# Moving a split, a tail transpose, thresholds and reciprocals in a fused attention and MLP kernel

## The chip, the cores and the metric

The kernel runs on one core of a Trainium2 chip. A core has five engines with instruction queues of their own: TensorE (PE in the profile; its weight loads are PEld), VectorE (DVE), ScalarE (ACT), GpSimd (POOL) and SyncE (SP, which here only issues transfers). Data lies in SBUF and PSUM, 128 partitions each; transfers to and from HBM and transposing transfers run on 16 DMA engines. The metric is the device time of one execution in microseconds (us).

## The reference

Eight batches of eight heads, 576 positions, head size 64. Scores below the row's maximum less `tau` (0.02) are cut off, the rest goes through a softmax and multiplies `v`; the heads are joined, and a two-layer MLP follows:

```python
scores = scale * np.matmul(q, k.transpose(0, 1, 3, 2))          # 8 x 8 x 576 x 576
thresh = np.max(scores, axis=-1, keepdims=True) - tau
scores = np.where(scores >= thresh, scores, -1e9)
attn = np.exp(scores - np.max(scores, axis=-1, keepdims=True))
attn = attn / (np.sum(attn, axis=-1, keepdims=True) + 1e-09)
out = np.matmul(attn, v)                                        # -> x: 4608 x 512
h = x @ w_in                                                    # 512 x 2048
return np.maximum(0.01 * h, h) @ w_out                          # 2048 x 512
```

## The kernel before

**Data.** `q` and `k` come as fp32 and are split into two fp16 parts, a high one (64 times the value, rounded) and a low one (what is left), so that the scores are the sum of three fp16 products (high by high, low by high, high by low). A unit of this work is one batch, one pair of heads and `q` or `k`: a tile `raw` of 128 x 512 elements. The 512 first positions of a batch are its main part; the 64 last ones of all heads are its *tails*, loaded as the tile `rawt` of 128 x 256.

**Splitting.** There are two ways. `split_pool` (L496) does it on POOL alone: scale (L137), cast to the high part (L143), subtract (L147). `split_now` (L150) does it on ACT (high, L157) and DVE (low, L158), in two instructions each per unit. After the split, `turn` (L161) transposes the 16 (for tails 8) blocks on PE into a PSUM tile `tp` with the tag "h", of which there are two buffers, and copies them by ACT or DVE into `kT` or `qT` (L179, L187). The first 64 columns of `kT` are tails, and a second copy of them goes to columns 576 to 640 (L184 for batch 0). `turn_rows` (L189) is the form for batches 2 to 7.

**Steps.** The attention is cut into 144 steps (18 per batch): 128 query rows of a pair of heads, or the tail rows of two pairs. One turn of the loop (L531) handles the scores of step n, the softmax of step n-1, the turning of the weights of earlier steps, and the MLP work that is queued (`l1q`, `l2q`: at most one `layer1` unit and two `layer2` units in a turn). Each engine executes its instructions in the order in which the program issues them. Within a turn:

- PE: `scores` (L244); `idle` matmuls on the identity in the first eleven turns (L505, they fill time and nothing reads them); the transposes of `turn` listed for that turn in `turns_at`; for the first eight steps the transposes of the weights (L323); `layer1` (L383), `layer2` (L399); the product with `v` of an earlier step, `pv` (L340).
- DVE: `copy_min` (L252, two instructions: scores out of PSUM, negated, with the row minimum as an accumulator), the threshold for n < 28 (L261), `weights` of step n-1 (L296: mask times exponential, with the row sum), the reciprocal of the sums (L302), copies out of PSUM, and x, the product with the reciprocal (L362).
- ACT: for one head the exponential (L287), for the other Prelu with the threshold as bias, then the exponential (L283, L284); L385 after `layer1`, L405 after `layer2`.
- POOL: what `pool_at` lists for the turn (splits, casts of `v`, weight loads `load_w`), the threshold for n >= 28 (L264), and `widen` (L305), which spreads the reciprocal to 64 columns for each head. Before turn 7, `widen` runs on DVE.
- SP: loads, stores, and from the ninth step on the transposing transfer of the weights of a pair of steps (L313), right after `widen`; the product with `v` follows three turns or more after the pair's `widen`.

**Start.** Before the loop, the first unit of `k` is loaded from SP's queue and the first of `q` from ACT's. The k tails follow on SP's queue as two transfers, then the second pair and all others. 34 `idle` matmuls run; `first` is the order of batch 0's units: (pair 0, k), (pair 0, q), (tails, k), (1, k), (1, q), (2, k), (2, q), (3, k), (3, q), (tails, q). The first three are split by `split_now` and turned ahead of the loop, with four `idle` matmuls before the tails. The second pair (1, k) and (1, q) is split by `split_now` in turn 0, between step 0's copies and step 1's. POOL splits (2, k) and (2, q) ahead of the loop, (3, k) and (3, q) in turns 0 and 1, the q tails in turn 6:

```python
for key in first[5:7]:
    split_pool(key)
for n_, key in zip((0, 1, 6), first[7:]):
    at(pool_at, n_, lambda key=key: split_pool(key))
for i in range(8):
    at(pool_at, 2 + i // 2 if i < 4 else i, lambda i=i: load_w(i))
```

**Reciprocals.** For the first eight steps the sums of each step are inverted alone (`n == 1` in `recip`). From then on it is once per pair of steps (`n == 2`, 128 x 4 elements), 68 times in all, on DVE, and POOL widens the result.

Of the kernel before, what the change touches and what calls it, by code (L numbers as in the profile page):

```python
# [37 lines left out]
def kernel(  # L38
# [24 lines left out]
    ident = sb.tile([128, 128], FP16, name="ident")  # L63
    minus_tau = sb.tile([128, 1], FP32, name="minus_tau")


# [15 lines left out]

    def load_tails(b, which, eng=None):
        t = sb.tile([128, 2, 2, 64], FP32, tag="rawt", bufs=2, name="rawt")
        src = SRC[which][b, :, MAIN:S, :].rearrange("(u sh) p d -> u p sh d", u=2)
        for u in range(2):
            (eng or nc.sync).dma_start(out=t[ds(64 * u, 64), :, :, :].rearrange("p s h d -> p (s h) d"), in_=src[u])
        tails[b, which] = t
# [61 lines left out]
    def split_now(key):  # L150
        t = halves[key] = new_half()
        for i in range(2):
            if key[1] == "t":
                src, n = tails[key[0], key[2]][:, :, i, :], 2
            else:
                src, n = pair_of(*key)[:, i, :, :], 4
            nc.scalar.activation(out=t[:, 0, 0:n, i, :], in_=src, func=AF.Copy, bias=0.0, scale=64.0)  # L157
            nc.vector.scalar_tensor_tensor(out=t[:, 1, 0:n, i, :], in0=src, scalar=64.0, in1=t[:, 0, 0:n, i, :],  # L158
                                           op0=AX.mult, op1=AX.subtract)

    def turn(key, copy=None):  # L161
        copy = copy or nc.scalar.copy
        b, p, which = key
        dst, half = turned_of(b, which), halves.pop(key)
        n = 2 if p == "t" else 4
        c0 = 0 if which == "q" else 64
        if p == "t":
            c0 = MAIN if which == "q" else 0
            tp = ps.tile([128, 2, 2, 2, 64], FP16, tag="h", bufs=2, name="tp")
        else:  # L170
            tp = ps.tile([128, 2, 4, 128], FP16, tag="h", bufs=2, name="tp")
        for x in range(2):
            for t in range(n):
                for h in range(2):
                    o = tp[ds(64 * h, 64), x, :, t, :] if p == "t" else tp[ds(64 * h, 64), x, t, :]
                    nc.tensor.transpose(o, half[:, x, t, h, :], ident[:, :])
        if p == "t":
            for x in range(2):
                copy(out=dst[:, x, :, ds(c0, 64)], in_=tp[:, x, :, :, :].rearrange("d u s p -> d (u s) p"))  # L179
            if which == "k" and b:  # L180
                nc.gpsimd.tensor_copy(out=dst[:, :, :, 576:640], in_=dst[:, :, :, 0:64])
            elif which == "k":
                for x in range(2):
                    nc.vector.tensor_copy(out=dst[:, x, :, 576:640],  # L184
                                          in_=tp[:, x, :, :, :].rearrange("d u s p -> d (u s) p"))
        else:
            copy(out=dst[:, :, p, ds(c0, 512)], in_=tp[:, :, :, :].rearrange("d x t p -> d x (t p)"))  # L187
# [68 lines left out]
    def threshold(st):  # L256
        st.th = sb.tile([128, 2, 2], FP32, tag="th", bufs=3, name="th")
        if st.n < 28:

            least = sb.tile([128, 1], FP32, tag="least", bufs=2, name="least")  # L260
            nc.vector.tensor_scalar(out=st.th[:, :, 0], in0=st.mn[:, :, 0], scalar1=tau_f, scalar2=None, op0=AX.add,  # L261
                                    op1=AX.min, accum_out=least[:, :])
        else:
            nc.gpsimd.tensor_scalar(out=st.th[:, :, 0], in0=st.mn[:, :, 0], scalar1=1.0, scalar2=tau_f, op0=AX.mult,  # L264
                                    op1=AX.add)
# [34 lines left out]
    def recip(pr, c, n):  # L300
        pr.rec = sb.tile([128, 2, 2], FP32, tag="rec", bufs=2, name="rec")
        nc.vector.reciprocal(out=pr.rec[:, 0:n, :], in_=pr.sum[:, ds(c, n), :])  # L302

# [157 lines left out]
    masks.make_identity(nc, ident[:, :])  # L461
    nc.gpsimd.memset(minus_tau[:, :], -tau_f)

    def load_pair(p, which, eng):
# [6 lines left out]
    load_pair(0, "q", nc.scalar)  # L471
    load_tails(0, "k", nc.sync)
    load_pair(1, "k", nc.sync)
# [4 lines left out]
    for s in range(2):  # L478
        load_v(0, s)
        if s == 0:  # L480
            load_vtails(0)
    load_tails(0, "q", nc.sync)
    for t in v16:
# [29 lines left out]
    turn(first[1], nc.vector.tensor_copy)  # L513
    idle(4)
    turn(first[2])
    idle(5)
    for key in first[5:7]:
        split_pool(key)
    for n_, key in zip((0, 1, 6), first[7:]):
        at(pool_at, n_, lambda key=key: split_pool(key))  # L520
    for i in range(8):
        at(pool_at, 2 + i // 2 if i < 4 else i, lambda i=i: load_w(i))
    at(turns_at, 0, lambda: turn(first[3]))
    for n_, key in zip((1, 2, 3, 4, 8), first[5:]):
        at(turns_at, n_, lambda key=key: turn(key, nc.vector.tensor_copy if key[2] == "q" else None))
# [5 lines left out]
    while n < N + 7 or l1q or l2q or stores:  # L531
# [8 lines left out]
        if n == 0:  # L540
            split_now(first[3])
            threshold(steps[0])
            split_now(first[4])
        if n == 1:
# [72 lines left out]
```

## Time and profile before

| | before |
|---|---|
| median of 3 runs | 500.94 us (500.85 to 500.95) |
| profiled execution | 500.9 us, span 499.1 us |
| PE busy | 475.7 us, 95% |
| DVE busy | 414.3 us, 83% |
| ACT busy | 433.1 us, 87% |
| POOL busy | 305.5 us, 61% |
| granted TensorE clock, mean | 0.996 |
| time of the DMA packets, queue q1 (loads, stores, transposes) | 80.5% of 16 engines |

The profile is of one execution. A line such as `L252 DVE TENSOR_SCALAR_CACHE_REDUCE s<-sc 128x576` names the program line, the engine, the operation, output and input tiles and shape; then come busy time and the mean duration of one in ns, and the idle time of the engine just before with what ended it. In an answer in order of time the first two numbers are the start and the length in us, and a bracket gives the idle time before with what ended it. `DVE_READ_ACCUMULATOR` and `ACTIVATION_READ_ACCUMULATOR` are the second half of an instruction that also gives a sum or a minimum. In a table of stages the numbers are the engine's busy time in that stage, and PEclk is the granted clock, 1.00 at full speed. The chain of waits is followed back from the last instruction, at each step to what released it.

### The profile page before, as it was taken

What the parts mean: (1) busy time and instruction counts of PE and PEld (TensorE: products, weight loads), DVE (VectorE), ACT (ScalarE), POOL (GpSimd) and SP (SyncE); (2) the same over time, 40 slices, a digit from 0 to 9 for tenths busy, and PEclk for the clock granted to TensorE, in tenths of its full rate; (3) what the DMA queues carried; (4) which work ended last, traced back from release to release, by engine and by line L of the source; (5) the groups of instructions that cost most, each with busy time, mean ns of one, the idle gap of its engine ahead of it and who ended that gap; (6) DMA issues with size and microseconds to landing.
All of it is one profiled execution on the core that took longest, in us unless ns stands there. A gap on an engine that the chain in (4) does not pass through costs nothing.

```text
span 499.1 us, 19695 instructions
## 1 busy us (share of the span) xinstructions
PE 475.7 (95%) x8043; PEld 344.4 (69%) x8043; DVE 414.3 (83%) x1228; ACT 433.1 (87%) x785; POOL 305.5 (61%) x517
## 2 busy tenths in 40 slices
PE   7878789989999999999999999999999999999996
PEld 6556566656677777777777777777777777667884
DVE  4999999998989898998989898998989898878100
ACT  4998987898999999999999999999999999999431
POOL 4973687557867687666867687666867683322000
PEclk9989999999999999999999999999999999999999
DMA  8897898899998999999997999999898969767512
GB/s 246 238 202 121 156 193 175 144 205 189 217 168 182 193 204 211 186 165 220 191 185 172 203 199 199 195 172 210 197 200 153 205 148 158 138 117 144 126 45 65
DMA packets 220443, 87.79 MB, mean 176 GB/s; under 512 B 190656, under 2 KB 217280, under 8 KB 220352
## 3 DMA queue, kind: packets, MB, share of 16 engines
q1 hardware_dynamic: 217392, 82.07, 80.5%
q0 software_dynamic: 2688, 4.19, 4.8%
q8 instruction: 63, 1.03, 0.9%
q10 hardware_dynamic: 272, 0.26, 0.2%
q14 instruction: 28, 0.23, 0.1%
HBM read 36.70 MB, written 9.44 MB: 92 GB/s over the span
## 4 chain that ended last, share of the span: by engine, by line
PE 80%; DVE 11%; ACT 3%; DMA 2%; issue 1%; POOL 1%; SPq 0%; DVEq 0%; POOLq 0%; ACTq 0%
PE hp L383 26%; PE o L399 20%; PE sc L244 20%; PE pv L340 7%; DVE s L252 5%; PE osc L399 3%; DVE w L296 3%; PE tpr L199 3%; DMA wT<-w 2%; DMA rawt<-in_k_dram 1%; DVE x L362 1%; ACT wT L325 1%; ACT s L283 1%; DVE half L158 1%; ACT e L287 1%
## 5 line engine op out<-in xcount | busy, mean ns | idle before, releaser
L252 DVE TENSOR_SCALAR_CACHE_REDUCE s<-sc 128x576 f32<-128x576 f32 x288 | 206.4, 754 | 32.6 <-PE sc L244 31.4
L244 PE MATMUL sc<-kT,qT 64*128 64x288 f16 (+1 forms) x1920 | 135.8, 286 | 4.0 <-DVE s L252 3.2
L383 PE MATMUL hp<-x,win 128*64 128x256 f16 x2048 | 136.5, 275 | 1.1 <-DVE x L362 1.0
L383 PEld LDWEIGHTS <-win 128*64 128x64 f16 x2560 | 118.5, 109 | 24.0 <-issue 18.1
L399 PE MATMUL o<-wout,g 128*64 128x512 f16 x992 | 127.8, 379 | 0.0
L296 DVE SCALAR_TENSOR_TENSOR w<-s,th,e 128x576 f16<-128x576 f32 x144 | 122.2, 849 | 0.5 <-ACT e L287 0.5
L244 PEld LDWEIGHTS <-qT 64*128 64x128 f16 (+1 forms) x1920 | 77.0, 97 | 58.6 <-issue 44.2
L264 POOL TENSOR_SCALAR th<-mn 128x2 f32<-128x2 f32 x116 | 53.5, 461 | 103.3 <-DVE s L252 76.9
L284 ACT ACTIVATE w<-s,minus_tau 128x576 f16<-128x576 f32 x144 | 111.7, 776 | 5.2
L283 ACT ACTIVATE s<-s,th 128x576 f32<-128x576 f32 x144 | 110.4, 766 | 2.0 <-POOL th L264 1.4
L287 ACT ACTIVATE e<-s,mn 128x576 f16<-128x576 f32 x144 | 110.2, 766 | 0.6 <-DVE s L252 0.5
L385 ACT ACTIVATE g<-hp 128x512 f16<-128x512 f32 x144 | 84.2, 585 | 29.3 <-PE hp L383 28.8
L399 PEld LDWEIGHTS <-g 128*64 128x64 f16 x1152 | 65.1, 110 | 30.1 <-issue 0.5
L147 POOL TENSOR_TENSOR half<-scaled,half 128x512 f16<-128x512 f32 (+1 forms) x75 | 82.2, 1096 | 1.1
L340 PE MATMUL pv<-wT,v 128*64 128x256 f16 (+1 forms) x960 | 52.1, 247 | 2.6 <-DMA wT<-w 2.6
L340 PEld LDWEIGHTS <-v 128*64 128x64 f16 x960 | 41.6, 111 | 15.8 <-issue 3.0
L137 POOL TENSOR_SCALAR scaled<-raw 128x512 f32<-128x512 f32 x60 | 43.7, 728 | 7.1 <-DMA raw<-in_k_dram 6.1
L305 POOL CAST w<-rec 128x256 f16<-128x256 f32 (+1 forms) x70 | 27.9, 398 | 31.4 <-DVE rec L302 31.0
L143 POOL CAST half<-scaled 128x512 f16<-128x512 f32 (+1 forms) x75 | 43.2, 576 | 4.6
L106 POOL CAST v<-vraw 128x256 f16<-128x256 f32 x64 | 34.4, 565 | 1.4
L362 DVE TENSOR_TENSOR x<-pv,wT 128x256 f16<-128x256 f32 x64 | 27.1, 423 | 3.5 <-PE pv L340 3.5
L284 ACT ACTIVATION_READ_ACCUMULATOR w<-s,minus_tau 128x1 f32 x144 | 26.9, 187 | 0.0
(52 smaller groups left out, 327.8 us busy)
## 6 DMA issues: line engine op xcount, KB each, us to landing
vraw<-in_v_dram SPq DMA_DIRECT2D x16, 512.0 KB, 5.4
out_dram<-osb SPq DMA_DIRECT2D x16, 512.0 KB, 3.4
raw<-in_k_dram SPq DMA_DIRECT2D x14, 512.0 KB, 4.7
raw<-in_q_dram SPq DMA_DIRECT2D x14, 512.0 KB, 5.3
win<-in_moe_w_in_dram POOLq DMA_DIRECT2D x4, 512.0 KB, 8.5
wout<-in_moe_w_out_dram POOLq DMA_DIRECT2D x4, 512.0 KB, 12.8
wT<-w SPq DMA_TRANSPOSE x68, 6.0
raw<-in_k_dram SPq DMA_DIRECT2D x4, 256.0 KB, 4.7
```

Of the source, the lines that this page charges most:

```text
L147: nc.gpsimd.tensor_tensor(out=halves[key][:, 1, 0:n, :, :], in0=scaled.pop(key)[:, 0:n, :, :], in1=halves[key][:, 0, 0:n, :, :], op=AX.sub ...
L244: nc.tensor.matmul(out=o, lhsT=lhs, rhs=turned[st.b, "k"][rows, kx, pair, ds(key0, 288)], start=(i == 0), stop=(i == 2), skip_group_check= ...
L252: nc.vector.tensor_scalar(out=st.s[:, h, :].rearrange("p (a b) -> p a b", a=2), in0=st.sc[h][:, :, 0:288], scalar1=-1.0 / UNIT, scalar2=No ...
L264: nc.gpsimd.tensor_scalar(out=st.th[:, :, 0], in0=st.mn[:, :, 0], scalar1=1.0, scalar2=tau_f, op0=AX.mult, op1=AX.add)
L283: nc.scalar.activation(out=z, in_=z, func=AF.Prelu, bias=st.th[:, h, 0:1], scale=-1.0, alpha=1e20)
L284: nc.scalar.activation(out=st.w[h], in_=z, func=AF.Exp, bias=minus_tau[:, :], scale=1.0, accum_out=st.sum[h])
L287: nc.scalar.activation(out=st.e[:, :], in_=st.s[:, h, :], func=AF.Exp, bias=st.mn[:, h, 0:1], scale=-1.0)
L296: nc.vector.scalar_tensor_tensor(out=st.w[0], in0=st.s[:, 0, :], scalar=st.th[:, 0, 0:1], in1=st.e[:, :], op0=AX.is_le, op1=AX.mult, accum ...
L340: nc.tensor.matmul(out=o, lhsT=v16[st.b % 2][:, 2 * c + u if st.tail else st.p, blk, :], rhs=rhs, start=(i == 0), stop=(i == 4), skip_grou ...
L383: nc.tensor.matmul(out=hp[ds(64 * u2, 64), jj, :], lhsT=w_in16[:, i, ds(128 * j + 64 * u2, 64)], rhs=g.x[:, i, :], start=(i == 0), stop=(i ...
L385: nc.scalar.activation(out=g.g[:, ds(nj * u, nj), :], in_=hp[:, :, :], func=AF.Prelu, bias=0.0, scale=1.0, alpha=0.01)
L399: nc.tensor.matmul(out=g.o[ds(64 * u2, 64), :], lhsT=g.g[:, j, ds(128 * m + 64 * u2, 64)], rhs=w_out16[:, j, :], start=(j == 0), stop=(j = ...
```

## The change

Four things change.

1. **Second pair.** (1, k) and (1, q) are no longer split by ACT and DVE in turn 0, but by POOL ahead of the loop, and (2, k) after them; (2, q), (3, k), (3, q) and the q tails follow in turns 0, 1, 2 and 6. The weight loads of POOL's queue are spread anew over turns 0 to 7. (1, k) is copied out of PSUM by DVE, not ACT; (3, q) is turned in turn 5, not 4.
2. **Tails.** The second transfer of the first k tails goes out on ACT's queue. `split_now` takes tails in one instruction per engine, and `turn` copies tails in one instruction for both parts, where there were two. The first k tails are turned in the PSUM buffer with the tag "o", and the four `idle` matmuls before them are dropped.
3. **Early thresholds.** For n < 28 DVE adds a tile `tau2` of two columns to the two minima (`scalar_tensor_tensor`, 1.0 times the first plus the second), where it was an add with a constant and an accumulator that nothing read.
4. **Reciprocals.** With `n == 2` the sums are raised to the power of -1 on POOL (`tensor_tensor` with `pow` against a tile of -1), right ahead of `widen` on the same engine.

```diff
+    tau2 = sb.tile([128, 2], FP32, name="tau2")
+    minus_one = sb.tile([128, 2, 2], FP32, name="minus_one")
...
-    def load_tails(b, which, eng=None):
+    def load_tails(b, which, engs=(nc.sync, nc.sync)):
...
-            (eng or nc.sync).dma_start(out=t[ds(64 * u, 64), :, :, :].rearrange("p s h d -> p (s h) d"), in_=src[u])
+            engs[u].dma_start(out=t[ds(64 * u, 64), :, :, :].rearrange("p s h d -> p (s h) d"), in_=src[u])
...
     def split_now(key):
         t = halves[key] = new_half()
-        for i in range(2):
+        for i in range(1 if key[1] == "t" else 2):
             if key[1] == "t":
-                src, n = tails[key[0], key[2]][:, :, i, :], 2
+                src = tails[key[0], key[2]][:, :, :, :]
+                hi, lo = (t[:, x, 0:2, :, :] for x in range(2))
             else:
-                src, n = pair_of(*key)[:, i, :, :], 4
-            nc.scalar.activation(out=t[:, 0, 0:n, i, :], in_=src, func=AF.Copy, bias=0.0, scale=64.0)
-            nc.vector.scalar_tensor_tensor(out=t[:, 1, 0:n, i, :], in0=src, scalar=64.0, in1=t[:, 0, 0:n, i, :],
-                                           op0=AX.mult, op1=AX.subtract)
-
-    def turn(key, copy=None):
+                src = pair_of(*key)[:, i, :, :]
+                hi, lo = (t[:, x, :, i, :] for x in range(2))
+            nc.scalar.activation(out=hi, in_=src, func=AF.Copy, bias=0.0, scale=64.0)
+            nc.vector.scalar_tensor_tensor(out=lo, in0=src, scalar=64.0, in1=hi, op0=AX.mult, op1=AX.subtract)
+
+    def turn(key, copy=None, bank="h"):
...
-            tp = ps.tile([128, 2, 2, 2, 64], FP16, tag="h", bufs=2, name="tp")
+            tp = ps.tile([128, 2, 2, 2, 64], FP16, tag=bank, bufs=2 if bank == "h" else 1, name="tp")
...
-            for x in range(2):
-                copy(out=dst[:, x, :, ds(c0, 64)], in_=tp[:, x, :, :, :].rearrange("d u s p -> d (u s) p"))
+            src = tp[:, :, :, :, :].rearrange("d x u s p -> d x (u s) p")
+            copy(out=dst[:, :, :, ds(c0, 64)], in_=src)
...
-                for x in range(2):
-                    nc.vector.tensor_copy(out=dst[:, x, :, 576:640],
-                                          in_=tp[:, x, :, :, :].rearrange("d u s p -> d (u s) p"))
+                nc.vector.tensor_copy(out=dst[:, :, :, 576:640], in_=src)
...
         if st.n < 28:
-            least = sb.tile([128, 1], FP32, tag="least", bufs=2, name="least")
-            nc.vector.tensor_scalar(out=st.th[:, :, 0], in0=st.mn[:, :, 0], scalar1=tau_f, scalar2=None, op0=AX.add,
-                                    op1=AX.min, accum_out=least[:, :])
+            nc.vector.scalar_tensor_tensor(out=st.th[:, :, 0], in0=st.mn[:, :, 0], scalar=1.0, in1=tau2[:, :],
+                                           op0=AX.mult, op1=AX.add)
...
-        nc.vector.reciprocal(out=pr.rec[:, 0:n, :], in_=pr.sum[:, ds(c, n), :])
+        if n == 2:
+            nc.gpsimd.tensor_tensor(out=pr.rec[:, :, :], in0=pr.sum[:, :, 0:2], in1=minus_one[:, :, :], op=AX.pow)
+        else:
+            nc.vector.reciprocal(out=pr.rec[:, 0:n, :], in_=pr.sum[:, ds(c, n), :])
...
+    nc.gpsimd.memset(tau2[:, :], tau_f)
+    nc.gpsimd.memset(minus_one[:, :, :], -1.0)
...
-    load_tails(0, "k", nc.sync)
+    load_tails(0, "k", (nc.sync, nc.scalar))
...
-    load_tails(0, "q", nc.sync)
+    load_tails(0, "q")
...
-    idle(4)
-    turn(first[2])
+    turn(first[2], bank="o")
     idle(5)
-    for key in first[5:7]:
+    for key in first[3:6]:
         split_pool(key)
-    for n_, key in zip((0, 1, 6), first[7:]):
+    for n_, key in zip((0, 1, 2, 6), first[6:]):
         at(pool_at, n_, lambda key=key: split_pool(key))
     for i in range(8):
-        at(pool_at, 2 + i // 2 if i < 4 else i, lambda i=i: load_w(i))
-    at(turns_at, 0, lambda: turn(first[3]))
-    for n_, key in zip((1, 2, 3, 4, 8), first[5:]):
+        at(pool_at, i if i < 2 else 1 + i // 2 if i < 6 else i, lambda i=i: load_w(i))
+    at(turns_at, 0, lambda: turn(first[3], nc.vector.tensor_copy))
+    for n_, key in zip((1, 2, 3, 5, 8), first[5:]):
         at(turns_at, n_, lambda key=key: turn(key, nc.vector.tensor_copy if key[2] == "q" else None))
...
         if n == 0:
-            split_now(first[3])
             threshold(steps[0])
-            split_now(first[4])
```

## The prediction

> **What bounds the kernel now.** I read the page's engine table first. It makes PE the busiest engine, and DVE, ACT and POOL look covered:
>
> ```profile
> PE 475.7 (95%) x8043; PEld 344.4 (69%) x8043; DVE 414.3 (83%) x1228; ACT 433.1 (87%) x785; POOL 305.5 (61%) x517
> ```
>
> That is an average, so the busy times by stage came next (columns: length; PE, PEld, DVE, ACT, POOL busy; PE clock; DMA share; GB/s):
>
> ```profile
> 10.00:15.00 5.00, 3.41 (x57) 2.31 (x53) 4.81 (x11) 1.99 (x4) 4.70 (x7) 1.00 1.00 238
> 30.00:35.00 5.00, 5.00 (x76) 3.70 (x77) 4.83 (x13) 4.03 (x8) 4.86 (x6) 0.66 1.06 203
> 65.00:70.00 5.00, 3.45 (x72) 2.82 (x67) 4.83 (x15) 4.51 (x9) 4.81 (x8) 1.00 1.25 152
> 140.00:200.00 60.00, 60.00 (x1104) 43.69 (x1104) 53.83 (x155) 55.40 (x102) 43.20 (x74) 1.00 0.99 191
> 200.00:300.00 100.00, 100.00 (x1724) 71.95 (x1722) 90.39 (x265) 92.78 (x171) 71.34 (x121) 1.00 0.94 191
> ```
>
> There are two regimes. Until some 120 us DVE is full (4.8 of 5) and PE has holes; from then on PE is full nearly to the end. Whatever the first 120 us lose or win goes to the end one for one; work taken off DVE later is worth nothing, because PE hides it. The start in order of time:
>
> ```profile
> 7.11 0.99 ACT L187 COPY kT<-tp 128x1024 f16<-128x1024 f16 x1
> 8.16 0.41 PE L176 MATMUL tp<-ident,half 128*64 128x128 f16 x8 [0.81 <-ACT kT L187]
> 8.85 0.62 POOL L137 TENSOR_SCALAR scaled<-raw 128x512 f32<-128x512 f32 x1 [6.09 <-DMA raw<-in_k_dram]
> 11.35 0.62 POOL L137 TENSOR_SCALAR scaled<-raw 128x512 f32<-128x512 f32 x1
> 11.55 1.44 DVE L158 SCALAR_TENSOR_TENSOR half<-raw,half 128x256 f16<-128x256 f32 x2
> 13.49 1.01 ACT L187 COPY kT<-tp 128x1024 f16<-128x1024 f16 x1 [3.01 <-PE tp L176]
> ```
>
> The first k tails wait for a PSUM buffer (PE 0.81 us behind ACT's copy). The second pair's splits sit on DVE between two steps' copies while POOL waits 6.09 us for input; from its first split to the second is 2.50 us. POOL's queue then:
>
> ```profile
> 34.41 0.83 POOL L492 DMA_DIRECT2D wout<-in_moe_w_out_dram  x1
> 40.11 0.29 POOL L305 CAST w<-rec 128x128 f16<-128x128 f32 x1 [4.87 <-DVE rec L302]
> ```
>
> After unbroken work POOL stands idle for 4.87 us: room for two more splits. Last, the chain of waits in the middle:
>
> ```profile
> 68.36 0.19 DVE rec L302
> 68.55 0.03 POOLq L305
> 68.58 0.36 POOL v L111
> 68.94 0.05 issue
> 68.98 0.02 POOLq L143
> 69.00 0.40 POOL w L305
> 69.40 0.60 POOL half L147
> 70.00 7.57 DMA wT<-w
> 77.57 0.04 issue
> 77.61 0.74 PE pv L340 x10
> ```
>
> Here POOL, then the transposing DMA, hold PE: a GpSimd reciprocal ahead of that widening is in this chain.
>
> **The change, part by part.**
>
> *Tails.* The second half of the k tails is issued on ACT's queue: 0.70 us (half of the 1.41 us of two issues) off SP's queue, so all later loads issue 0.7 us earlier. ACT's table load moves back by that, ending at 3.2 instead of 2.52, still ahead of the first data at 4.19. ACT's split of the tails (6.70 before) starts near 6.0 as one instruction, its k copy near 6.4 instead of 7.11. In their own bank the tails are transposed without the 0.81 us wait. Their copies become one each: ACT between its 0.37 for 256 columns and 1.00 for 1024, say 0.55; DVE 0.42, as its 512-column copies (L209). Scores end near 8.9 instead of 10.18. The four dropped idle matmuls (0.40 us) lay in a wait: nothing.
>
> *Second pair.* Four ACT splits (0.41 each) and four DVE ones (11.55 to 15.03, partly waiting) go; DVE gains the k copy (0.68 as its q copies), ACT loses its own (1.00). POOL does k1, q1, k2 first. k1 lands 4.7 us (median of these loads) after an issue now at 2.0, so 6.7 to 7.4; at 2.5 us each the three are ready at 9.2 to 9.9, 11.7 to 12.4, 14.2 to 14.9. Step 1's scores stand behind k1's transposes: 10.7 to 11.6, its row copies at 11.6 instead of 14.96, 3.3 us early. But step 2's scores now stand behind the transposes of k2, which POOL had done by 11.4 before and now has only at 14.9: with 0.65 of transposes and 0.91 of scores they end at 16.4 against 17.96, and DVE's copies start at 16.4 against 18.41. So 3.3 shrinks to about 2. q2 (17.4) and k3 (20.8, behind a weight issue of 0.6) come just in time for the following steps; q3 (26.5) is why its turn is moved from step 4 to 5, which moves 0.68 us of DVE by a step. POOL ends its early block at 35.24 + 2 x 2.5 - 1.5 to 2.2 = 38.0 to 38.7: still before the 40.11 less 2 at which step 6's reciprocal will want it, or just behind; DVE's next dependent copy stood at 42.88, with 1.7 us to spare. The weight loads go out up to 4 us earlier (0.6 to 0.8 of POOL each, already counted as POOL's work); landing 8.5 us later, the first four are long there when the first `hp` stands at 49.24: nothing, and if the DMA share of about 1 then holds back a raw load by as much, the start ends at its lower bound. The two new memsets (0.1 each) lie in POOL's 6.09 us wait. The V casts that move behind two weight issues and a split end near 23.5, for a first pv that stood at 26.29. Start: **-2.0**. Bounds: -0.7, if each split takes 2.75 as beside busy DVE (the third, from 13.97 to 16.71, did) and k1 lands at 7.4, to -3.3, if step 1's lead holds.
>
> *Thresholds.* 28 times a 0.154 us instruction and a 0.083 us accumulator read become one two-term sum. No row shows it at two elements; a 128x2 reciprocal takes 0.17. So at most the 0.08 read goes, at least nothing. Eight lie on the chain after 50 us: **-0.6** (0 to -0.6; nearest is the two-element row).
>
> *Reciprocals.* 68 leave DVE (0.177 each). From 120 us on nothing is won. Before, four lie on the chain with DVE next: 49.45 (0.17), 55.67 (0.27), 88.21 (0.26), 100.75 (0.15): **-0.85**. POOL gains one `pow` of 128x4 (price P) ahead of each widening, and all behind it: the splits, thresholds from step 28 on, for which ACT's Prelu waits, and SP's transposes. No row shows P. Nearest by size is the threshold on POOL, 128x2: mean 0.461, 0.19 at least; nearest by operands the two-input 128x512 row, 1.162. I take 0.46 and keep 0.19 to 1.16. At 62.3 it replaces a reciprocal with its waits (+0.2), at 69.0 it comes on top (+0.46): **+0.66** (+0.1 to +2.1). In the PE-bound part POOL has 28.66 us idle in 100 us, at 3.09 us a step (row copies from 50.44 to 455.28, 131 steps) 16.2 pairs: 1.77 us a pair. P = 0.46 hides there.
>
> By the Trainium skill, page "GPSIMD Engine Reference", section 3 ("Performance versus the Vector engine"), GpSimd is some 2x slower on two-input arithmetic: as an estimate P = 0.35 and the sum 0.2 lower. It says nothing of a power.
>
> *Merged tail copies.* Two of 0.28 become one of 0.42, twice on the chain: **-0.3**.
>
> *Clock.* From 30.8 to 34.2 PE ran at half clock, after 1.91 us of idle up to 29.91; step 6's scores took 1.62 instead of 0.91, and DVE waited for it, some 1.2 us in all. Idle stretches move now: I leave the dip in and put +-1.2 into the range.
>
> By "TensorE: Matmul & The Clock Gate" of the Trainium skill, Part 1, "What's actually happening", only an idle window of about 3.4 us slows PE. This trace has the dip after 1.91 us, so the row decides; by the page there would be no dip and the sum 1.2 lower.
>
> Sum: 500.9 (the profiled execution; span 499.1 and 1.8 around it) - 2.0 - 0.6 - 0.85 + 0.66 - 0.3 = **497.8**. The median of the runs, 500.94, is the same within 0.1.
>
> **Rivals.**
>
> *POOL becomes the bound* (slower). Place: `pow` in front of every widening. It decides at P = 1.77 us: beyond, POOL has over 100% of the PE-bound part, and each of its 55 pairs or so (340 us by 6.18) pays the excess. P = 2.0 gives 497.8 - 0.66 + 3.75 in the middle + 0.23 x 55 = about 513; P = 2.5 about 542. For: a power is no plain arithmetic, and no row prices it. Against: four elements a partition, where 512 of a two-input operation take 1.16.
>
> *The start's gain is paid back* (no change). Two splits later on POOL, k2's and q2's turns hold PE, step 6's widening comes late, and the chain from 69 on is POOL and a 7.57 us DMA which move little. With nothing won at the start and P = 1.16: 500.9 - 0.6 - 0.85 - 0.3 + 2.1 = 501.3. For: POOL works 4.8 of 5 us at 65 to 70. Against: its 4.87 us wait at 35 to 40.
>
> *All of it counts* (much faster). Step 1's lead of 3.3 holds, and in the DVE-full stretch every freed piece shortens a step: 13 reciprocals with their waits of 0.28, 28 reads of 0.08, 0.3: 9.5 in all, 491.4. For: DVE 4.8 of 5. Against: ACT is as full from 15 to 30, and PE's waits for `wT` stay.
>
> **How the numbers follow.** Forecast 0.60 (own range 495 to 499.9: the sum with two of its open terms at their ends), POOL bound 0.16, paid back 0.14, all counts 0.10. No change is within 0.2%, 1.0 us, which is what a measurement can tell. Faster: 0.57 + 0.10; within: 0.02 and 0.10 of the second rival; slower: 0.16 + 0.04 + 0.01. The range 493 to 502 leaves out the POOL bound and the far third of the fast case.
>
> **What would show it.** Right: step 1's row copies near 11.6 and step 2's near 16.4; a wait of PE for POOL's `half` in between; no DVE split after 9 us; POOL's idle at 35 to 40 nearly gone; `pow` at 0.2 to 1.2; PE full from some 115 on, at an unchanged 3.09 us a step. Wrong: a `pow` over 1.8, ACT's Prelu waiting for POOL, a PE with holes after 140, or half clock at another place of the start.

## The result, and the profile after

The changed kernel takes 509.07 us (median of 4 runs, 508.77 to 509.22) against 500.94 us: a ratio (of the means of the runs) of 1.0159, with a 95% interval of 1.0142 to 1.0177. It is slower by 8.0 us (7.1 to 8.9), where 497.8 was forecast and 502 was the upper end. Its profiled execution took 509.1 us, with a span of 507.2.

The engine table of the changed kernel:

```profile
PE 478.9 (94%) x8039; PEld 346.2 (68%) x8039; DVE 428.3 (84%) x1124; ACT 429.4 (85%) x778; POOL 385.5 (76%) x593
```

DVE has 104 instructions fewer and is busy 14 us *longer*, so some of its instructions became longer. POOL gained 80 us for 76 instructions; 69 us of them are the 68 powers. The busy times by stage of the changed kernel (columns as before):

```profile
10.00:15.00 5.00, 3.73 (x74) 2.59 (x74) 4.78 (x11) 2.38 (x5) 4.70 (x7) 1.00 1.14 277
30.00:35.00 5.00, 3.86 (x76) 3.18 (x74) 3.83 (x11) 3.66 (x7) 4.79 (x10) 0.83 1.04 187
35.00:40.00 5.00, 2.51 (x36) 1.79 (x32) 4.83 (x12) 2.84 (x5) 3.78 (x5) 0.85 1.22 200
65.00:70.00 5.00, 4.56 (x99) 3.87 (x100) 4.83 (x12) 4.76 (x10) 4.75 (x7) 1.00 1.02 150
200.00:300.00 100.00, 99.96 (x1738) 71.58 (x1736) 92.78 (x245) 92.07 (x170) 88.03 (x136) 1.00 0.94 191
```

In the middle POOL goes from 71 to 88 of 100 and is still not full, DVE from 90.4 to 92.8 although its reciprocals are gone, and PE still reads as full. The start of the changed kernel, in order of time:

```profile
7.44 0.59 ACT L182 COPY kT<-tp 128x512 f16<-128x512 f16 x1
10.58 0.91 PE L245 MATMUL sc<-kT,qT 64*128 64x288 f16 x12
11.53 0.76 DVE L253 TENSOR_SCALAR_CACHE_REDUCE s<-sc 128x576 f32<-128x576 f32 x1
14.49 0.41 PE L179 MATMUL tp<-ident,half 128*64 128x128 f16 x8 [0.82 <-POOL half L149]
14.83 0.91 PE L245 MATMUL sc<-kT,qT 64*128 64x288 f16 x12
16.09 0.74 DVE L253 TENSOR_SCALAR_CACHE_REDUCE s<-sc 128x576 f32<-128x576 f32 x1
```

Step 1's row copies stand at 11.53 and step 2's at 16.09, where 11.6 and 16.4 were forecast, with the forecast wait for POOL's `half` in between. So up to step 2 the forecast of the times holds. At step 2 that is in part luck: the scores had ended at 15.74, and the row copies stood behind DVE's own queue, a threshold of 0.96 us from 13.49 and `weights` of 1.25 from 14.37, which the forecast does not have. How far each step's row copies stand from those of the kernel before (us; worked out from the starts of the row copies in both traces):

| step | 1 | 2 | 4 | 5 | 6 | 7 | 8 | 28 | 72 | 143 |
|---|---|---|---|---|---|---|---|---|---|---|
| after | -3.4 | -2.3 | -1.7 | -1.2 | +0.1 | +1.5 | +2.6 | +4.7 | +6.3 | +8.2 |

Five of the test kernels below start as the kernel before (`pow_only`, `mul_only`, `pow_late`, `th_dve`, `pow_th_dve`), and at step 1 they stand 0.0 to 0.8 us ahead of it: in such a table less than 1 us is not to be told from the difference between two executions. The time is lost in three places: 4.9 us between steps 2 and 8, 2.1 from there to step 28, and 3.5 over the last 115 steps, where nothing but the reciprocals differs. In the chain of waits of the changed kernel the place of POOL is plain:

```profile
123.87 1.03 POOL rec L302
124.95 0.40 POOL w L307
125.35 1.12 POOL half L149
126.55 0.58 POOL th L263
137.10 0.99 POOL rec L302
138.15 0.60 POOL w L307
138.75 1.12 POOL half L149
139.96 0.20 POOL th L263
140.19 0.78 ACT s L282
```

From 123.87 to 140.16 the chain never leaves POOL's queue; powers, widenings, splits and thresholds stand one behind the other until a threshold lets ACT's Prelu go. Before, between 100 and 140 us, POOL held the chain from 106.25 to 109.30 only; it begins and ends with these pieces:

```profile
106.25 0.63 POOL th L264
109.10 0.20 POOL th L264
109.33 0.79 ACT s L283
```

From 154.8 to 460 us the chain of the changed kernel is PE's alone, as it is before, though its steps stay longer. So the chain shows POOL in the way up to 140 us and cannot say what makes the later steps longer.

### The profile page after: what moved, and what is told of

Same layout as the page of the kernel before. It is cut to its first block, busy times and chain, and to the rows that moved or that the text cites. A ratio compares the mean times of both kernels' runs of the same rounds, so it can differ in the third digit from the quotient of the medians.

```text
span 507.2 us, 19614 instructions
## 1 busy us (share of the span) xinstructions
PE 478.9 (94%) x8039; PEld 346.2 (68%) x8039; DVE 428.3 (84%) x1124; ACT 429.4 (85%) x778; POOL 385.5 (76%) x593
## 4 chain that ended last, share of the span: by engine, by line
PE 70%; POOL 3%; ACT 3%; DVE 2%; issue 1%; POOLq 0%; DVEq 0%
PE hp L385 23%; PE o L401 18%; PE sc L245 17%; PE pv L342 6%; PE osc L401 3%; PE tpr L200 3%; DVE s L253 1%; ACT w L283 1%; DVE w L295 1%; ACT s L282 1%; POOL half L149 1%; POOL rec L302 1%; POOL th L263 0%; ACT e L286 0%; ACT g L387 0%
## 5 line engine op out<-in xcount | busy, mean ns | idle before, releaser
L295 DVE SCALAR_TENSOR_TENSOR w<-s,th,e 128x576 f16<-128x576 f32 x144 | 141.4, 982 | 0.7 <-ACT e L286 0.4
L385 PEld LDWEIGHTS <-win 128*64 128x64 f16 x2560 | 119.7, 109 | 25.5 <-issue 20.8
L263 POOL TENSOR_SCALAR th<-mn 128x2 f32<-128x2 f32 x116 | 56.8, 490 | 45.3 <-DVE s L253 38.0
L401 PEld LDWEIGHTS <-g 128*64 128x64 f16 x1152 | 66.4, 110 | 29.3 <-issue 0.5
L149 POOL TENSOR_TENSOR half<-scaled,half 128x512 f16<-128x512 f32 (+1 forms) x77 | 84.9, 1103 | 1.2
L302 POOL TENSOR_TENSOR rec<-sum,minus_one 128x4 f32<-128x4 f32 x68 | 69.2, 1017 | 15.5 <-ACT s L282 7.6
L145 POOL CAST half<-scaled 128x512 f16<-128x512 f32 (+1 forms) x77 | 48.0, 624 | 4.9
L139 POOL TENSOR_SCALAR scaled<-raw 128x512 f32<-128x512 f32 x62 | 40.4, 652 | 5.0 <-DMA raw<-in_k_dram 3.9
L307 POOL CAST w<-rec 128x256 f16<-128x256 f32 (+1 forms) x70 | 34.9, 499 | 9.2 <-DVE rec L304 4.9
L108 POOL CAST v<-vraw 128x256 f16<-128x256 f32 x64 | 33.2, 549 | 1.4
```

The source lines that it names most:

```text
L149: nc.gpsimd.tensor_tensor(out=halves[key][:, 1, 0:n, :, :], in0=scaled.pop(key)[:, 0:n, :, :], in1=halves[key][:, 0, 0:n, :, :], op=AX.sub ...
L295: nc.vector.scalar_tensor_tensor(out=st.w[0], in0=st.s[:, 0, :], scalar=st.th[:, 0, 0:1], in1=st.e[:, :], op0=AX.is_le, op1=AX.mult, accum ...
L302: nc.gpsimd.tensor_tensor(out=pr.rec[:, :, :], in0=pr.sum[:, :, 0:2], in1=minus_one[:, :, :], op=AX.pow)
L385: nc.tensor.matmul(out=hp[ds(64 * u2, 64), jj, :], lhsT=w_in16[:, i, ds(128 * j + 64 * u2, 64)], rhs=g.x[:, i, :], start=(i == 0), stop=(i ...
L401: nc.tensor.matmul(out=g.o[ds(64 * u2, 64), :], lhsT=g.g[:, j, ds(128 * m + 64 * u2, 64)], rhs=w_out16[:, j, :], start=(j == 0), stop=(j = ...
```

## The experiments

Each run's ratio is to the kernel before on the same chip, and a difference in us is that ratio times 501.

| kernel | ratio | interval | us |
|---|---|---|---|
| after | 1.0159 | 1.0142 to 1.0177 | +8.0 |
| before with the two-term threshold (sum_only) | 1.0038 | 1.0023 to 1.0053 | +1.9 |
| before with the power (pow_only) | 1.0069 | 1.0054 to 1.0084 | +3.5 |
| before with second pair and tails (start_only) | 1.0032 | 1.0017 to 1.0046 | +1.6 |
| after without the two-term threshold (no_sum) | 1.0115 | 1.0100 to 1.0130 | +5.8 |
| after without the power (no_pow) | 1.0053 | 1.0034 to 1.0071 | +2.7 |
| pow_only with a product (mul_only) | 0.9981 | 0.9966 to 0.9995 | -1.0 |
| pow_only, power a turn later (pow_late) | 1.0215 | 1.0181 to 1.0248 | +10.8 |
| before, all thresholds on DVE (th_dve) | 1.0225 | 1.0204 to 1.0247 | +11.3 |
| th_dve with the power (pow_th_dve) | 1.0048 | 1.0024 to 1.0072 | +2.4 |
| before with a plain add (plain_add) | 1.0049 | 1.0034 to 1.0064 | +2.5 |
| before with the tails part (tails_only) | 1.0007 | 0.9994 to 1.0020 | +0.4 |
| start_only, last q unit turned in turn 4 (q3_at_4) | 0.9995 | 0.9980 to 1.0009 | -0.3 |
| tails part and one unit of the pair moved (one_unit) | 0.9979 | 0.9966 to 0.9992 | -1.1 |
| the same again (one_again) | 0.9985 | 0.9971 to 0.9998 | -0.8 |

### The three parts alone, and taken out

The first question was which part carries the 8 us. Thresholds alone:

```diff
-            nc.vector.tensor_scalar(out=st.th[:, :, 0], in0=st.mn[:, :, 0], scalar1=tau_f, scalar2=None, op0=AX.add,
-                                    op1=AX.min, accum_out=least[:, :])
+            nc.vector.scalar_tensor_tensor(out=st.th[:, :, 0], in0=st.mn[:, :, 0], scalar=1.0, in1=tau2[:, :],
+                                           op0=AX.mult, op1=AX.add)
```

> The kernel before with the two-term threshold alone. Theory A (a two-term sum on VectorE waits while GpSimd runs a two-input operation: 28 of them took 0.518 us on average in the changed kernel, 0.16 when nothing held them, 1.0 to 1.1 when they began inside a GpSimd subtract and ended with it): a mean near 0.5 us, and 28 x (0.52 - 0.23), about 8 us of VectorE's time in the stretch where VectorE is full, of which more than half shows: 504 to 509. Rival B (the loss is GpSimd's load at the start): thresholds alone cost nothing, 500 to 501.5.

Reciprocals alone:

```diff
-        nc.vector.reciprocal(out=pr.rec[:, 0:n, :], in_=pr.sum[:, ds(c, n), :])
+        if n == 2:
+            nc.gpsimd.tensor_tensor(out=pr.rec[:, :, :], in0=pr.sum[:, :, 0:2], in1=minus_one[:, :, :], op=AX.pow)
+        else:
+            nc.vector.reciprocal(out=pr.rec[:, 0:n, :], in_=pr.sum[:, ds(c, n), :])
```

> The kernel before with GpSimd's power alone. Theory A: the power takes 1.02 us, 68 times; in the changed kernel the steps drifted by 3.8 us from step 28 to the last one, so here about 3 to 4 us from there, and before step 28 between -2 (13 reciprocals off VectorE) and +2 (GpSimd late with the widening): 502 to 506, ScalarE's Prelu waiting for GpSimd's threshold some 20 us in all. Rival B: GpSimd's idle time of 1.77 us a pair takes 1.02 in without loss, 499 to 501.5.

The start alone is the changed kernel with both of these diffs undone:

> The changed kernel with thresholds and reciprocals as before: only the second pair's split on GpSimd and the tails. Theory A: the start's lead, 3.4 us at step 1 and 2.3 at step 2 in the changed kernel, is not eaten by thresholds: about 2 us are kept, 498 to 500. Rival B (two more splits make GpSimd late, and PE, waiting for it, falls to half clock): the lead is gone by step 7, 501 to 504, with half clock between 28 and 42 us as in the changed kernel.

The changed kernel with only the first diff undone:

> The changed kernel with the thresholds as before, the rest changed. Theory A: the thresholds cost 4 to 8 us, so 501 to 505. Rival B: 508 to 509.

And with only the second undone:

> The changed kernel with the reciprocals back on VectorE. Theory: the power's drift after step 28 (3.8 us) goes, and with it the thresholds are held less often: 503.5 to 505, the steps after 28 at the pace of the kernel before. Rival (in the changed kernel the first 28 steps alone make the loss): 507 to 509.

Each of the three parts alone makes the kernel slower: +1.9, +3.5, +1.6, together 7.0 of the 8.0. Taken out of the changed kernel, the sum is worth 2.2 and the power 5.3 (the intervals of these differences reach about 1.2 us to each side), so the power costs somewhat more in company than alone. The rows show where: before step 28 `pow_only` loses nothing, but the changed kernel stands at +4.7 there and `no_pow` at +2.4, and of the 28 two-term sums 17 take over 0.3 us with the power and 10 without it. By steps, `sum_only` loses between steps 5 and 16 (-0.1 to +2.55) and little later, `pow_only` is 0.3 *ahead* at step 28 and loses 3.6 after it, and `start_only` goes from -3.3 at step 1 to +3.1 at step 8.

### Why a shorter threshold costs time

The threshold was forecast to lose its 0.083 us accumulator read. Its rows when asked by its line (counts, then shortest, median and longest in ns), first before:

```profile
L261 DVE TENSOR_SCALAR_CACHE_REDUCE th<-mn x28: 139/155/156, 12.9 to 102.8; 128x2 f32<-128x2 f32 x28
```

then after:

```profile
L260 DVE SCALAR_TENSOR_TENSOR th<-mn,tau x28: 160/479/1129, 10.6 to 106.8; 128x2 f32<-128x2 f32 x28
```

Undisturbed it does take 0.16, but half of them take three times as much. What the long ones have in common shows in the order of time of the changed kernel:

```profile
25.19 1.15 POOL L149 TENSOR_TENSOR half<-scaled,half 128x512 f16<-128x512 f32 x1
25.35 1.02 DVE L260 SCALAR_TENSOR_TENSOR th<-mn,tau 128x2 f32<-128x2 f32 x1
...
35.26 1.17 POOL L149 TENSOR_TENSOR half<-scaled,half 128x512 f16<-128x512 f32 x1
35.35 1.10 DVE L260 SCALAR_TENSOR_TENSOR th<-mn,tau 128x2 f32<-128x2 f32 x1
```

An add of two elements that starts while POOL's subtract runs ends about 0.02 us after it (26.37 after 26.34, 36.45 after 36.43). To see whether the second operand tile is to blame or the loss of the accumulator, the before kernel got an add with constants alone and no accumulator:

```diff
-            nc.vector.tensor_scalar(out=st.th[:, :, 0], in0=st.mn[:, :, 0], scalar1=tau_f, scalar2=None, op0=AX.add,
-                                    op1=AX.min, accum_out=least[:, :])
+            nc.vector.tensor_scalar(out=st.th[:, :, 0], in0=st.mn[:, :, 0], scalar1=1.0, scalar2=tau_f, op0=AX.mult,
+                                    op1=AX.add)
```

> The kernel before with the early threshold as an add of a constant: one tile in, no accumulator. Theory A (VectorE's instruction is held by GpSimd because it reads two tiles from SBUF): with one input it is never held, some 0.15 us each, and without the 0.08 us read 0 to 1 us are won: 500 to 501. Rival (what the accumulator kept away is the wait: any small VectorE add from SBUF to SBUF without one is held while GpSimd works): a mean of 0.3 us or more with cases of 1 us, 501.5 to 503, as with the two-term sum.

It is as slow as the sum (+2.5 against +1.9, which the intervals do not part), and its row is held too:

```profile
L260 DVE TENSOR_SCALAR th<-mn x28: 168/170/1471, 12.3 to 103.4; 128x2 f32<-128x2 f32 x28
```

So the accumulator that nothing read was what kept the threshold free of POOL: with it the longest of 28 took 0.156. The sizes fit the times: in `sum_only` the 28 sums take 0.301 us on average and in `plain_add` 0.324, against 0.237 for the add and its read, which is 1.8 and 2.4 us more of DVE. The Trainium skill says this on the page "SBUF — State Buffer", section "Who interferes with whom": VectorE and GpSimd share one pair of ports, whoever is first has it for its whole instruction, and what wants it on VectorE is an instruction with two SBUF inputs (against a GpSimd instruction that reads SBUF), or a copy, cast or `tensor_scalar` ("not the form that also writes out its accumulator") whose operands meet the conditions for using both ports. The traces agree on the sum, the plain add and the form with the accumulator. They do not agree that every POOL instruction that reads SBUF holds DVE for its whole length: the power does not, as the next section shows.

### What in the power costs time

One power takes 1.02 us. To part its duration from its place in the queue, the same instruction with a product in place of the power:

```diff
-            nc.gpsimd.tensor_tensor(out=pr.rec[:, :, :], in0=pr.sum[:, :, 0:2], in1=minus_one[:, :, :], op=AX.pow)
+            nc.gpsimd.tensor_tensor(out=pr.rec[:, :, :], in0=pr.sum[:, :, 0:2], in1=minus_one[:, :, :], op=AX.mult)
```

> As the kernel with the power alone, but the sums are multiplied by -1 instead of raised to the power of -1, so the output is not the attention; what is timed is the same operands on the same engine. Theory A1 (the power itself is dear): the product takes 0.2 to 0.3 us instead of 1.02, and with 0.75 us of GpSimd a pair given back the drift of 3.6 us after step 28 goes: 500 to 501.5. Rival (moving the reciprocal behind GpSimd's queue is dear whatever it is): 503 to 505 as with the power.

Groups of instructions of `pow_only`, then of `mul_only` (busy us, then mean ns of one):

```profile
L304 POOL TENSOR_TENSOR rec<-sum,minus_one 128x4 f32<-128x4 f32 x68 | 69.2, 1018 | 14.8 <-DVE w L297 6.7 <-ACT e L288 3.7 <-ACT w L285 3.2
```

```profile
L304 POOL TENSOR_TENSOR rec<-sum,minus_one 128x4 f32<-128x4 f32 x68 | 13.5, 199 | 21.1 <-DVE w L297 10.9 <-ACT e L288 5.9 <-ACT w L285 1.9
```

The product takes 0.20, and with it the move off DVE *gains* 1.0 us (0.3 to 1.7). The profile of `mul_only` is of its slowest run (501.8 us, the median is 499.6), and even there the row copies lose nothing after step 28 (+1.1 there, +0.8 at the end). So moving the reciprocal was right, and the length of the power is the whole loss: 4.4 us between the two kernels for 68 times 0.82 us of POOL. Two consequences of the long instruction show in the trace from 140 to 440 us. One is ACT's Prelu waiting for POOL's threshold; before, after and `mul_only` in turn (total us, times, longest):

```profile
ACT s L283 <- POOL th L264: 0.4, 2, 0.2
```

```profile
ACT s L282 <- POOL th L263: 19.8, 29, 1.6
```

```profile
ACT s L284 <- POOL th L265: 1.0, 2, 0.5
```

The other is DVE's `weights`, which reads two SBUF tiles and meets POOL's reads as the two-term sum does. The same three kernels and stretch:

```profile
L296 DVE SCALAR_TENSOR_TENSOR w<-s,th,e x97: 807/811/1020, 141.5 to 438.8; 128x576 f16<-128x576 f32 x97
```

```profile
L295 DVE SCALAR_TENSOR_TENSOR w<-s,th,e x96: 805/814/1749, 140.2 to 438.3; 128x576 f16<-128x576 f32 x96
```

```profile
L297 DVE SCALAR_TENSOR_TENSOR w<-s,th,e x98: 805/811/1214, 139.5 to 439.5; 128x576 f16<-128x576 f32 x98
```

The longest is 0.94 us over the shortest, the mean goes from 0.822 to 1.009 (0.832 with the product), and 31 of 96 take over 0.9 us, where it was 5 of 97 before and with the product. It is tempting to put that down to the power itself, but the rows of the changed kernel say otherwise:

```profile
131.12 1.02 POOL L302 TENSOR_TENSOR rec<-sum,minus_one 128x4 f32<-128x4 f32 x1
131.79 0.81 DVE L295 SCALAR_TENSOR_TENSOR w<-s,th,e 128x576 f16<-128x576 f32 x1
...
150.28 1.16 POOL L149 TENSOR_TENSOR half<-scaled,half 128x512 f16<-128x512 f32 x1
150.30 1.75 DVE L295 SCALAR_TENSOR_TENSOR w<-s,th,e 128x576 f16<-128x576 f32 x1
```

All 18 `weights` that began while a power ran (0.6 us or more after its start) took 0.807 to 0.811 us. Of the 31 long ones 25 began during POOL's subtract of a split and ended 0.61 to 0.62 us after it, four did the same with a widening, and none ran beside a power. So the power does not hold `weights`, as the expectations below still suppose. It moves what follows it in POOL's queue, and the subtracts now lie where `weights` starts. `weights` in all takes 141.4 us instead of 122.2, the early thresholds 14.5 instead of 6.6; less 12 us of reciprocals, that is why DVE is busier.

Which of the two, the Prelu's waits or the held `weights`, carries the 3.6 us after step 28? A first attempt moved the power behind the threshold in POOL's queue, by finishing a pair one turn later:

```diff
+    late = []
+
+    def finish():
+        while late:
+            pr = late.pop(0)
+            recip(pr, 0, pr.n)
+            widen(pr, 0, pr.n)
+            turn_w(pr)
...
+        finish()
...
-                recip(last.pair, 0, last.pair.n)
-                widen(last.pair, 0, last.pair.n)
-                turn_w(last.pair)
+                late.append(last.pair)
+                if last.n < 28:
+                    finish()
```

> The kernel with the power alone, but from step 28 on the power, its widening and the transposing transfer of a pair are issued one turn later, behind that turn's threshold in GpSimd's queue. Theory R1 (the drift comes from the thresholds behind the power: ScalarE waited 19.5 us for them between 140 and 440 us): these waits go below 3 us and the drift of 3.6 us after step 28 to under 1: 500.5 to 502. Theory R2 (it comes from VectorE's weights held while the power runs, 1.00 us on average against 0.85): weights stay near 1.0 and the drift stays, 503.5 to 505. If the transfer a turn later makes PE wait for it, slower than 505.

The Prelu still waits 14.3 us in the same stretch, 9.7 us of waits of PE's weight load for the transposed weights `wT` come on top, and the loss after step 28 doubles to 7.4 us. Besides, 32 of the 68 powers begin there while `weights` runs, take 1.40 to 1.51 us and end 0.88 us after it. A cause was moved and others added, so this run decides nothing. A second attempt took the thresholds off POOL, in a control without and a kernel with the power:

```diff
-        if st.n < 28:
+        if st.n < N:
```

> The kernel before with all thresholds on VectorE, as an add with an accumulator. It is the control: 116 x 0.2 us more on VectorE, which has 9.6 us of 100 idle behind PE: 500.5 to 503.

> The same with the power on GpSimd. R1 (the drift is ScalarE waiting for GpSimd's thresholds): nothing waits for GpSimd but the widening, the power costs less than 1 us beside the control. R2 (VectorE's weights are held while the power runs): weights at 0.95 to 1.0 us on average against 0.85, and 3 us or more beside the control.

The control was expected to be nearly neutral and is 11.3 us slower: 116 thresholds of 0.155 and 0.083 are 27.6 us more for DVE. The stage from 200 to 300 us of `th_dve`, then of `pow_th_dve`:

```profile
200.00:300.00 100.00, 99.47 (x1714) 70.38 (x1712) 95.15 (x318) 90.38 (x166) 52.80 (x85) 1.00 0.92 186
```

```profile
200.00:300.00 100.00, 99.96 (x1726) 71.51 (x1722) 92.38 (x308) 91.60 (x170) 75.17 (x105) 1.00 0.91 190
```

With DVE at 95 of 100 the same power *gains* 8.9 us, while DVE loses 12 us of reciprocals (68 of 0.177); that DVE sets the steps there is the likely reason. Without a threshold of POOL the Prelu waits for POOL no more, the longest `weights` takes 1.22 us (1.26 in the control), and what is left against the kernel before after step 28 is 2.2 us. So the price of the power comes through what stands behind it in POOL's queue: thresholds that the Prelu waits for, and subtracts that hold `weights`. Its sign depends on what else is full. How the 3.6 us part between the Prelu's waits and the held `weights` stays open, because no run removed one and left the other.

### The start

What the tails part does alone (second transfer on ACT's queue, merged instructions, own bank, no `idle` before; the pair stays split by ACT and DVE):

> The kernel before with the tails' part alone. Theory: step 0's row copies are some 1.1 us earlier, as in the changed kernel, and VectorE, full from there on, carries the lead to the end: 499.6 to 500.2. Rival: step 1 waits for the second pair's splits as before, the lead is gone at step 2, 500.7 to 501.2.

Nothing at the end. By steps it is 1.6 us ahead at step 1, 0.5 at step 3, 0.2 behind at step 4, and within 0.4 us to either side from there on. POOL's first split starts at 8.75 us, where it was 8.85, so POOL is no earlier; that this is why the lead goes was not tested.

In `start_only` the lead of 3.3 us at step 1 is down to 0.3 at step 2. Its order of time and its stage there:

```profile
15.88 0.64 PE L179 MATMUL tp<-ident,half 128*64 128x128 f16 x8 [1.34 <-POOL half L149]
16.45 1.62 PE L245 MATMUL sc<-kT,qT 64*128 64x288 f16 x12
```

```profile
15.00:20.00 5.00, 4.12 (x48) 2.94 (x50) 2.74 (x9) 3.22 (x5) 4.75 (x7) 0.53 0.92 225
```

PE waits for POOL's third split and then does scores at half clock, 1.62 us instead of 0.91. That much belongs to this one execution: four other kernels have the same first four turns apart from thresholds, and their profiles keep a lead of 1.7 to 2.3 us at step 2 (the changed kernel, `no_sum`, `no_pow` and the one that follows). By step 5 all five leads are down to 0.5 to 1.7. The next loss is where the last q unit is turned. To test the move from turn 4 to turn 5 alone, `start_only` was given turn 4 back:

```diff
-    for n_, key in zip((1, 2, 3, 5, 8), first[5:]):
+    for n_, key in zip((1, 2, 3, 4, 8), first[5:]):
```

> The kernel of tails and second pair with the last q unit turned in step 4 again, not in 5. Theory (its copy stands behind step 5's weights in VectorE's queue, and step 6's scores waited 2.2 us for it): that wait goes, PE waits up to 1.5 us for GpSimd's split in step 4 instead, 500.5 to 502. Rival (its place is of no account): 502.2 to 503.2.

It is 1.9 us faster by the ratios, and 2.9 by the row copies of the last step. The line of the scores of step 6 in `start_only`, then in `q3_at_4`:

```profile
33.35 0.91 PE L245 MATMUL sc<-kT,qT 64*128 64x288 f16 x12 [2.23 <-DVE qT L188]
```

```profile
30.45 1.26 PE L245 MATMUL sc<-kT,qT 64*128 64x288 f16 x12
```

In turn 5 the copy of `qT` stands behind DVE's `weights` of the step before (1.21 us there), its reciprocal and widening, and PE stands idle for 2.23 us with step 6's scores next; in turn 4 there is no such wait. More follows in `start_only`: `weights` of 2.21 us from 35.85, and a granted clock of 0.65 from 38 to 42, where it is 1.00 in `q3_at_4`. Turn 4 has its price too: PE waits 1.23 us for POOL's split of that unit, and 1.7 us of the lead go between steps 4 and 5. So `q3_at_4` is only level with the kernel before. The last run moves one unit of the second pair instead of two, (1, q), leaves (1, k) with ACT and DVE, and keeps the tails part and every other order of before:

```diff
-    for key in first[3:6]:
+    for key in first[4:7]:
         split_pool(key)
-    for n_, key in zip((0, 1, 2, 6), first[6:]):
+    for n_, key in zip((0, 1, 6), first[7:]):
...
         if n == 0:
+            split_now(first[3])
             threshold(steps[0])
```

> The kernel before with the tails' part, and of the second pair only q split by GpSimd, ahead of (2, k) and (2, q); k by ScalarE and VectorE as before; weight loads and turns as before. Theory (in the changed kernel PE stands behind GpSimd's third split, three deep in its queue): the third split ends 2.5 us earlier relative to its use, PE waits for none, no half clock at 15 to 20 us, step 1 is 2 us early and keeps 1.5 to 2: 498.7 to 499.7. Rival (GpSimd is late even with one unit more): 500.5 to 502.

> The same kernel as with one unit of the second pair on GpSimd, measured again in more rounds: 0.996 to 0.999 of before if its 0.9979 holds, 1.000 if it was chance.

Both times it is faster than before and after: 0.9979 and 0.9985, intervals below 1, about 1 us. Its lead is 1.4 us at step 1 and 1.6 at step 28 (1.2 and 1.0 the second time): small, but it is kept. That the kernel keeps it because each later split moves back by one place in POOL's queue and not by two was not tested.

## Why the prediction was wrong

*What bounds the kernel.* Of the two regimes the first was read rightly: what `sum_only` and `start_only` lose before step 28 goes to the end nearly unchanged (by row copies 1.9 at step 28 and 2.5 at the end, 1.8 and 1.8). The second was not. "from then on PE is full ... work taken off DVE later is worth nothing, because PE hides it" fails in both directions: `th_dve` shows that 27.6 us of work more on DVE costs 11.3, and `pow_only` that 115 steps get 3.6 us longer while PE reads 99.96 of 100 (200 to 300 us). A PE that reads as full in this profile is not a cover of any size.

*Tails and merged copies* (-0.3, and a part of the start). Sizes right (ACT's copy 0.59 for 0.55, DVE's 0.42), worth nothing: +0.4 (-0.3 to +1.0).

*Second pair: -2.0, between -0.7 and -3.3.* Measured together with the tails and merged copies +1.6 (0.9 to 2.3): wrong in sign and outside the bounds. Right were the steps up to row copies of step 2. The step that failed is "q3 (26.5) is why its turn is moved from step 4 to 5, which moves 0.68 us of DVE by a step". It was costed at the length of the copy; what counts is what the copy stands behind on DVE and who waits for it, and the move to turn 5 cost 1.9 us. The rest is that the lead of the first steps did not last, as in the rival of a start that is paid back (its chance was 0.14). Of that rival's reasons one is seen, PE held by POOL's later splits (0.82 us at 14.49 and 0.75 at 17.39 in the changed kernel, 1.23 in `q3_at_4`); a late first widening is not, since POOL had 2.72 us of idle time ahead of it. How much each wait cost was not measured.

*Thresholds: -0.6, between 0 and -0.6.* Measured +1.9 (1.2 to 2.7). The failed step is "at most the 0.08 read goes, at least nothing": the instruction was priced by a short row that POOL never holds, and a loss was ruled out without a reason. What the runs showed instead: without the accumulator POOL's instructions hold it, for a mean of 0.301 us alone and 0.518 in the changed kernel, against 0.237 for both halves before.

*Reciprocals: -0.85 and +0.66.* Measured alone, the two together are +3.5 (2.7 to 4.2). The gain on DVE stands: with a product of 0.20 the move is worth -1.0. P was sized at 0.46 and is 1.017, inside the bounds 0.19 to 1.16. But the upper bound was carried only into the early chain. The step that failed is "1.77 us a pair. P = 0.46 hides there", and the rival built on it, "decides at P = 1.77": a power of 1.02 leaves POOL idle for 11 to 12% of the middle and yet costs 0.03 us a step, because idle time averaged over a pair does not lie where the instruction stands: between 140 and 440 us the Prelu's waits for POOL go from 0.4 to 19.8 us, and the `weights` over 0.9 us from 5 to 31. The prediction had named who is behind it, the thresholds from step 28 on "for which ACT's Prelu waits", and put no price on it.

*Clock: left in, within 1.2.* It moved, as allowed for: half clock from about 28.7 to 31.6 and from 38.9 to 42 in the changed kernel, and in `start_only` in part from 15 to 20 and from 38 to 42. It was listed as a sign that the forecast fails, and it was one.

*Signs.* Right: row copies of steps 1 and 2, PE's wait for `half`, no DVE split after 9 us, a power between 0.2 and 1.2. Half right: POOL's idle stretch at 35 to 40, 3.78 of 5 busy. Seen, of those called wrong: the Prelu waiting for POOL, half clock elsewhere. Not seen: steps at an unchanged 3.09 us (3.14 over the same 131 steps; over the last 115 it is 3.11 against 3.08).

## What to carry to other kernels

Price an instruction not only by its row but by what it shares: an accumulator that nobody reads can be what keeps a small VectorE instruction from waiting out a GpSimd one. Average idle time on an engine with a queue in order covers an added instruction only if that idle time lies between it and whoever waits for the next thing in that queue; look at who is behind it before looking at the share. And ahead of a move between engines, ask for the price of the very operation: a product and a power of the same four elements differ by a factor of five on GpSimd. When an instruction turns out longer, look at what the other engine runs in that very moment: the new instruction need not be what holds it.

## What the runs showed of the hardware that was not expected

- GpSimd's power of 128x4 fp32 takes 1.017 us (68 times), the product of the same operands 0.199.
- A VectorE instruction on two elements takes 0.16 or up to 1.47 us, with two inputs (`sum_only`) as with one and no accumulator (`plain_add`), by what GpSimd is doing; with an accumulator never over 0.157 in any run.
- `weights`, 128x576 with two inputs, goes from 0.81 to 1.75 us when it begins during GpSimd's 128x512 subtract, and stays at 0.81 when it begins 0.6 us or more into a power. The other way round, a power that begins during `weights` takes 1.40 to 1.51 us instead of 1.02 (32 times in `pow_late`).
- Half clock came after idle stretches of 1.91 us (before), 2.46 and 2.49 us (after). In these two lines of the changed kernel the same eight matmuls take 0.62 and, after the idle stretch, 1.01 us:

```profile
12.33 0.62 PE L509 MATMUL idle<-ident 128*128 128x128 f16 x8
28.72 1.01 PE L509 MATMUL idle<-ident 128*128 128x128 f16 x8 [2.46 <-DVE x L364]
```

After 2.23 us of idle time in `start_only` the scores ran at full clock (0.91). So the length of one stretch does not decide it here; what else does was not tried.
